# One tuned kernel, two parallel layers: loading the first 256 row pairs of A's input by plain copies with TensorE transposes, issuing the Q and K weight loads from SyncE, cutting the last odd rows in two column pieces, and new ranks

## The chip, the cores and the metric

The kernel runs on one core of one Trainium2 chip. The metric is the device time of one execution in microseconds (us). A kernel is run several times; the text quotes medians. Each execution also has a state. It is called slow when its granted TensorE clock is visibly below that of the other runs, or when it takes over 1.5% longer than the fastest run of the same kernel. Comparisons use fast runs only, and a difference under 2% counts as "same".

Engines in the profile: PE is TensorE's matmuls, PEld its weight loads, DVE is VectorE, ACT ScalarE, POOL GpSimd, SP SyncE (which here issues most of the DMAs). PSUM is the memory that TensorE writes; "evacuating" a PSUM tile means that VectorE or ScalarE copies it out, after which the buffer is free again.

## The reference

Two independent layers over 2048 rows of 448 columns, side by side in the output.

```python
def A(x, wqkv, wo):                 # x [1, 2048, 448], 16 heads of 28
    q, k, v = split(x @ wqkv)
    idx = pos[:, None] - 2 * arange(8)[None, :]        # 8 keys, every second row back
    logits = einsum("bhsd,bhswd->bhsw", q, k[idx]) * 28 ** -0.5      # masked where idx < 0
    return einsum("bhsw,bhswd->bhsd", softmax(logits), v[idx]) @ wo

def B(x, Lambda, B, C, log_dt, Dskip):                 # a linear recurrence, 448 states
    Lam_bar = exp(exp(log_dt) * Lambda)
    h[t] = Lam_bar * h[t - 1] + ((Lam_bar - 1) / Lambda * B) @ x[t]
    return 2 * real(C @ h) + x * Dskip

out = concatenate([A(...), B(...)], axis=-1)           # bfloat16
```

## The kernel before

Rows are handled as 1024 pairs: one row of the working layout holds an even and an odd row of x, 896 values. Matmuls need x with its columns on the partitions, so `xA` holds x transposed, seven slabs of 128. All of it came by DMA transposes, 128 row pairs at a time ("a tile" below), issued by SyncE. V and Q/K are products of two row-tiled matmuls that run side by side: "a pair".

```python
    def xbar_x(dst, src, lo, hi):
        SP.dma_start_transpose(dst[:, :, lo:hi], src[lo:hi, :])
    # ...
    xbar_x(xA, xA2, 0, 128)                                # x tile 0, transposed by the DMA
    ACT.dma_start(Wv[:, 0:3, :], wmain(2))                 # V's weights
    ACT.dma_start(Wv[0:64, 3, :], A_wqkv[384:448, 2 * D:3 * D])
    ACT.dma_start(Wraw[0:64, 3, :], A_wqkv[384:448, 0:2 * D])
    # ... small parameters
    for i in range(1, 4):
        xbar_x(xA, xA2, 128 * i, 128 * i + 128)
    ACT.dma_start(Wraw[:, 0:3, D:2 * D], wmain(1))         # K's weights, from ScalarE
    # ...
    ACT.dma_start(Wraw[:, 0:3, 0:D], wmain(0))             # Q's weights
    # ...
    def n_vw(e):                                           # copies of Wv for the second row tile
        V.tensor_copy(Wv[64:128, 3, :], Wv[0:64, 0, :])
        V.tensor_copy(Wv[0:64, 4:7, :], Wv[64:128, 0:3, :])
        V.tensor_copy(Wv[64:128, 4:7, :], Wv[0:64, 1:4, :])
    # ...
    def evac(e, o, i):                                     # from PSUM, on either engine
        if e == "A":
            ACT.copy(o, i)
        else:
            V.tensor_copy(o, i)
    # ... the last odd rows of B (t == 7): one PSUM unit, two halves of columns
        def half(e, lo, hi, h=h):
            evac(e, h["o"][:, 1, lo:hi], h[1][:, 1, lo:hi])
        # ...
        n3 = [node(f"ye{t}{1 + i}", {"AV"[i]: 0.3}, lambda e, i=i, half=half: half(e, 224 * i, 224 * i + 224), [n1, n2], r, frees=[(n1, 0)])
              for i in range(2)]
    # ... and before everything, a warm-up of TensorE with throw-away matmuls
    for i in range(11):
        PE.matmul(ps[:, 0, :], zz[:, 0:128], zz[:, 128:640], start=True, stop=True)
```

The order of the instructions is not written by hand. Every piece of work is a node with a cost on each engine that can do it; a small list scheduler runs through the nodes at build time, always taking the ready node with the lowest rank, and thereby fixes each engine's order and which engine evacuates what. The 22 pairs of numbers in `RANK` tune it.

## Time and profile before

| | before |
|---|---|
| median of the first three runs | 135.64 us (135.48 to 136.37) |
| span of the profiled execution | 136.1 us |
| time of that same execution | 138.0 us, state slow, mean granted clock 0.983 |
| TensorE busy in it | 127.0 us (93%) |

How to read it: TensorE is the busiest engine, so whatever leaves it idle, or makes it run at a lower clock, is what a change can gain. The prediction below shows the slices and stretches.

```profile
span 136.1 us, 3771 instructions
```

The span covers less than the timed duration (a later fast run: 133.9 against 135.86, about 2 less). A span of 136.1 is therefore an execution of about 138, and no run of the three quoted took that long.

### The profile page before, as it was taken

Reading aid. Unit: us, or ns where it says so; the run is one execution under the profiler, and the core shown is the slowest. Engines: PE = TensorE matmul, PEld = TensorE weight load, DVE = VectorE, ACT = ScalarE, POOL = GpSimd, SP = SyncE. Lnnn points to the kernel's source line nnn. Section 1 sums busy time; section 2 is a strip of 40 time slices with the busy share of each in tenths; the row PEclk is TensorE's granted clock in tenths of the full one; section 3 lists DMA queues with packets and bytes.
Section 4 is the critical chain, followed back from the end, with each engine's and each line's share of the span. In section 5 each row is a group of like instructions: output and inputs, shape, how many; then the busy total and the mean of one; then the engine's idle time right before and its main releaser. Section 6 shows DMA issues by size and latency. Waiting matters only on the chain.

```text
span 136.1 us, 3771 instructions
## 1 busy us (share of the span) xinstructions
PE 127.0 (93%) x1516; PEld 70.3 (52%) x1516; DVE 107.5 (79%) x191; ACT 88.2 (65%) x118; POOL 28.6 (21%) x109
## 2 busy tenths in 40 slices
PE   6849999999997999999999999999999999999980
PEld 2214567987434545445454545655666545455540
DVE  0505999999899799999999999999999999811110
ACT  0024999997999687699997889836766257511120
POOL 6965316401589900000000000000000010000000
PEclk9977999999999999999999999999999999999998
DMA  3999999791648939333313340089254765432121
GB/s 92 249 183 310 262 113 201 156 127 35 135 90 145 241 69 193 66 88 62 92 37 89 75 99 5 0 232 167 101 141 105 159 187 196 153 135 72 67 101 43
DMA packets 43938, 17.26 MB, mean 127 GB/s; under 512 B 35214, under 2 KB 43918, under 8 KB 43918
## 3 DMA queue, kind: packets, MB, share of 16 engines
q1 hardware_dynamic: 42448, 15.78, 53.7%
q10 hardware_dynamic: 1374, 1.21, 3.6%
q8 instruction: 13, 0.21, 0.7%
q14 instruction: 7, 0.06, 0.1%
q0 software_dynamic: 96, 0.00, 0.1%
HBM read 3.62 MB, written 3.67 MB: 54 GB/s over the span
## 4 chain that ended last, share of the span: by engine, by line
PE 72%; ACT 10%; DVE 7%; DMA 5%; issue 3%; SPq 1%; ACTq 0%
PE mm L528 21%; PE mm L778 14%; PE mm L970 8%; PE mm L979 8%; PE mm L737 5%; DMA xA<-in_A_x_dram 5%; PE mm L972 4%; PE mm L869 4%; PE mm L714 3%; PE mm L718 2%; ACT P L724 2%; DVE Va L507 2%; ACT wtmp L511 2%; ACT Kt L505 1%; ACT tab L454 1%
## 5 line engine op out<-in xcount | busy, mean ns | idle before, releaser
L724 ACT ACTIVATE P<-mm 128x896 bf16<-128x896 f32 (+1 forms) x36 | 31.4, 930 | 2.0 <-PE mm L718 1.9
L505 ACT CAST ys<-mm 128x896 bf16<-128x896 f32 (+2 forms) x16 | 12.2, 779 | 22.3 <-PE mm L979 8.9
L528 PE MATMUL mm<-xA,Wpad 64*128 64x256 bf16 (+1 forms) x168 | 26.4, 305 | 0.2 <-ACT Va L505 0.2
L529 PE MATMUL mm<-xA,Wpad 64*128 64x256 bf16 (+1 forms) x168 | 26.5, 305 | 0.0
L536 POOL MEMSET tick<- 1x1 f32 x40 | 5.0, 124 | 85.8 <-PE mm L529 85.6
L778 PE MATMUL mm<-xB,WT 128*128 128x512 bf16 x98 | 22.5, 379 | 0.5 <-ACT P L724 0.3
L528 PEld LDWEIGHTS <-Wpad 64*128 64x128 bf16 x168 | 15.3, 94 | 7.0 <-POOL tick L536 0.2
L528 PE MATMUL mm<-Wv,xA 64*128 64x448 bf16 x56 | 13.4, 378 | 2.5 <-DMA xA<-in_A_x_dram 2.2
L529 PEld LDWEIGHTS <-Wpad 64*128 64x128 bf16 x168 | 15.0, 94 | 0.8 <-issue 0.6
L778 PEld LDWEIGHTS <-WT 128*128 128x128 bf16 x98 | 9.1, 97 | 11.1 <-issue 0.9
L529 PE MATMUL mm<-Wv,xA 64*128 64x448 bf16 x56 | 13.4, 379 | 0.0
L970 PE MATMUL mm<-C,h 128*128 128x448 bf16 x56 | 11.9, 353 | 0.0
L979 PE MATMUL mm<-C,h 128*128 128x448 bf16 x56 | 11.9, 353 | 0.0
L528 PE MATMUL mm<-wo,OT 64*128 64x448 bf16 x56 | 10.8, 349 | 0.0
L529 PE MATMUL mm<-wo,OT 64*128 64x448 bf16 x56 | 10.8, 349 | 0.0
L744 DVE TENSOR_TENSOR O<-mm,rcs 112x896 bf16<-112x896 f32 (+1 forms) x9 | 9.8, 1092 | 0.3
L528 PEld LDWEIGHTS <-xA 64*128 64x128 bf16 x56 | 5.3, 100 | 7.3 <-DMA xA<-in_A_x_dram 3.2
L807 DVE TENSOR_TENSOR_SCAN rs<-p_r,ini,rv 128x512 bf16<-128x512 f32 x7 | 8.7, 1272 | 0.0
L737 PEld LDWEIGHTS <-P 128*128 128x128 bf16 x288 | 8.1, 96 | 1.3 <-issue 0.4
L1004 DVE TENSOR_TENSOR ys<-mm,xd 128x448 bf16<-128x448 f32 x3 | 1.9, 625 | 8.5 <-ACT ys L505 8.5
L807 DVE TENSOR_TENSOR_SCAN rs<-p_r,rv 128x512 bf16<-128x512 f32 x7 | 8.3, 1215 | 0.0
L505 ACT CAST u<-mm 128x1024 bf16<-128x1024 f32 (+1 forms) x6 | 5.2, 870 | 4.7 <-PE mm L778 4.5
(172 smaller groups left out, 243.0 us busy)
## 6 DMA issues: line engine op xcount, KB each, us to landing
out_dram<-ys SPq DMA_DIRECT2D x15, 224.0 KB, 2.4
Wraw<-in_A_wqkv_dram ACTq DMA_DIRECT2D x2, 336.0 KB, 5.2
wo<-in_A_wo_dram SPq DMA_DIRECT2D x2, 336.0 KB, 3.4
vw<-Va SPq DMA_DIRECT2D x2, 203.0 KB, 3.0
vw<-Va SPq DMA_DIRECT2D x2, 174.0 KB, 4.9
Wv<-in_A_wqkv_dram ACTq DMA_DIRECT2D x1, 336.0 KB, 3.4
natW<-in_B_B_re_dram SPq DMA_DIRECT2D x1, 336.0 KB
natW<-in_B_B_im_dram SPq DMA_DIRECT2D x1, 336.0 KB, 5.2
```

The lines of the kernel that those rows point to most:

```text
L505: ACT.copy(o, i)
L528: x = PE.matmul(ps[:, a, 0:n], lhs(0, lo[i]), rhs(0, lo[i]), start=(i == 0), stop=(i == 6), skip_group_check=True)
L529: y = PE.matmul(ps[:, b, 0:n], lhs(64, hi[i]), rhs(64, hi[i]), start=(i == 0), stop=(i == 6), skip_group_check=True)
L724: ACT.activation(P[:].rearrange("p s g q -> p g s q")[:, 2 * z:2 * z + 2, :, 0:n], h["s"][z][:, :, 0:4 * n].rearrange("p g (s q) -> p g s ...
L737: PE.matmul(av[:, par, 29 * hd:29 * hd + 29], hb_[par]["P"][:, hd // 4, hd % 4, :], v[:, par, hd, :], start=True, stop=True)
L744: V.tensor_tensor(O[0:n, :].rearrange("p (a h d) -> p a h d", a=2, h=H), avv[0:n, :, :, 0:DH], rc.unsqueeze(3).to_broadcast((n, 2, H, DH)) ...
L778: PE.matmul(ps[:, i, :], WT[:, j, 128 * m:128 * m + 128], xB[:, j, HALF * hf:HALF * hf + HALF], start=(j == 0), stop=(j == 6))
L807: V.tensor_tensor_scan(h["s"][:, i], p["r2"][:, k:k + 1].to_broadcast((128, HALF)), h["v"][:, i], 0.0 if hf == 0 else ini[:, m:m + 1], ALU ...
L869: PE.matmul(ps[0:n, i, 0:D], natW[:, m, D + 128 * k:D + 128 * k + n], lazy["C1"][:, m, :], start=(m == 0), stop=False, skip_group_check=True)
L970: PE.matmul(ps[:, 0, 0:D], hb[:, m, lo:lo + 128], lazy["C2"][:, m, :], start=(m == 0), stop=False, skip_group_check=True)
L972: PE.matmul(ps[:, 0, 0:D], xB[:, k, tk], Gm[:, k, :], start=False, stop=(k == 3), skip_group_check=True)
L979: PE.matmul(ps[:, 1, 0:D], hb[:, m, lo + 1:lo + 129], lazy["C1"][:, m, :], start=(m == 0), stop=(t in YD and m == 6), skip_group_check=True)
```

## The change

Its intent: the first stage of TensorE's work starts sooner and has no hole, because the first two tiles of x come by plain loads and TensorE, idle then anyway, transposes them; the K and Q weights leave ScalarE's queue, so that it has nothing to issue when evacuations start; and at the end less work follows the last matmul. All 22 ranks were retuned with it, and the warm-up falls from eleven matmuls to seven.

```diff
-    xbar_x(xA, xA2, 0, 128)
+    xn_ = [Pb[i][:].rearrange("p a b c -> p (a b c)")[:, 0:2 * D] for i in range(2)]
+    SP.dma_start(xn_[0], xA2[0:128, :])
     ACT.dma_start(Wv[:, 0:3, :], wmain(2))
     ACT.dma_start(Wv[0:64, 3, :], A_wqkv[384:448, 2 * D:3 * D])
-    ACT.dma_start(Wraw[0:64, 3, :], A_wqkv[384:448, 0:2 * D])
+    SP.dma_start(xn_[1], xA2[128:256, :])
 # ... (small parameters)
-    for i in range(1, 4):
+    for i in range(2, 4):
         xbar_x(xA, xA2, 128 * i, 128 * i + 128)
-    ACT.dma_start(rows[7:14, :], B_Lambda_re.rearrange("(c p) -> c p", p=64))
-    ACT.dma_start(Wraw[:, 0:3, D:2 * D], wmain(1))
-    for i in range(4, 6):
-        xbar_x(xA, xA2, 128 * i, 128 * i + 128)
-    ACT.dma_start(Wraw[:, 0:3, 0:D], wmain(0))
-    for i in range(6, 8):
+    SP.dma_start(Wraw[0:64, 3, :], A_wqkv[384:448, 0:2 * D])
+    SP.dma_start(Wraw[:, 0:3, D:2 * D], wmain(1))
+    xbar_x(xA, xA2, 512, 640)
+    SP.dma_start(Wraw[:, 0:3, 0:D], wmain(0))
+    for i in range(5, 8):
         xbar_x(xA, xA2, 128 * i, 128 * i + 128)
 # ... (B's x in two transposes instead of four; Wv's copies split into three nodes)
+    def n_xt(e, i, h):
+        h["ps"] = unit()
+        tp = h["tp"] = h["ps"][:].rearrange("p a b -> p (a b)").bitcast(BF16)
+        for k in range(7):
+            PE.transpose(tp[:, 1024 * (k // 4) + 128 * (k % 4):1024 * (k // 4) + 128 * (k % 4) + 128], xn_[i][:, 128 * k:128 * k + 128], eye[:])
+
+    def n_xe(e, i, z, h):
+        n = (4, 3)[z]
+        evac(e, xA[:, 4 * z:4 * z + n, 128 * i:128 * i + 128],
+             h["tp"][:, 1024 * z:1024 * z + 128 * n].rearrange("p (k n) -> p k n", k=n))
 # ... (nodes and dependencies for these; all 22 ranks)
+        def piece(e, lo, n, ds, tk=tk, h=h):
+            ps, hb = unit(), hbuf(1)
+            h["z", lo] = ps
+            for m in range(7):
+                PE.matmul(ps[:, 1, 0:n], hb[:, m, 385:513], lazy["C1"][:, m, lo:lo + n], start=(m == 0), stop=False, skip_group_check=True)
+ # ... (the skip term)
-            def half(e, lo, hi, h=h):
-                evac(e, h["o"][:, 1, lo:hi], h[1][:, 1, lo:hi])
+            for i, (lo, n, ds) in enumerate(((0, 320, (0, 1, 2)), (320, 128, (3,)))):
 # ... (piece, evacuation on VectorE or ScalarE, store, for each)
-    for i in range(11):
+    for i in range(7):
         PE.matmul(ps[:, 0, :], zz[:, 0:128], zz[:, 128:640], start=True, stop=True)
```

## The prediction

> **What bounds the kernel now.** I read the page first: engine totals and the 40 slices.
>
> ```profile
> PE 127.0 (93%) x1516; PEld 70.3 (52%) x1516; DVE 107.5 (79%) x191; ACT 88.2 (65%) x118; POOL 28.6 (21%) x109
> ...
> PE   6849999999997999999999999999999999999980
> DVE  0505999999899799999999999999999999811110
> ACT  0024999997999687699997889836766257511120
> PEclk9977999999999999999999999999999999999998
> ```
>
> TensorE is nearly full from slice 4 (13.6 us) to the end. VectorE and ScalarE are full only from slices 4 and 5 on, and PEclk has its one dip in slices 2 and 3. So the time is TensorE's work plus what is lost in the first 12 us and after its last matmul. Next, stretches of the start (TensorE busy, clock, DMA share, GB/s) and of all later time.
>
> ```profile
> 1.32:5.20 3.88, 3.88 (x10) 1.00 0.90 199
> 5.20:6.16 0.96, 0.52 (x4) 1.00 1.34 231
> 6.16:7.10 0.94, 0.93 (x8) 1.00 1.24 205
> 7.10:8.89 1.79, 0.00 (x0) 0.89 1.17 143
> 8.89:11.50 2.61, 2.61 (x14) 0.50 1.26 271
> ```
> ```profile
> 12.00:18.00 6.00, 6.00 (x72) 3.44 (x70) 5.62 (x27) 5.31 (x10) 1.86 (x9) 1.00 1.03 268
> 18.00:24.00 6.00, 5.60 (x88) 4.44 (x85) 5.85 (x18) 5.67 (x12) 2.75 (x12) 1.00 1.09 151
> 24.00:40.00 16.00, 16.00 (x223) 10.97 (x219) 15.32 (x26) 15.10 (x20) 6.16 (x28) 1.00 0.61 108
> 40.00:45.00 5.00, 4.16 (x36) 1.90 (x34) 4.64 (x7) 4.01 (x5) 4.92 (x15) 1.00 0.80 143
> 45.00:118.00 73.00, 72.75 (x997) 39.40 (x996) 70.35 (x109) 53.87 (x68) 4.20 (x22) 1.00 0.49 115
> ```
>
> The first 11 matmuls (1.32 to 5.7) are a dummy warm-up. The first V half-tile, four row-tiled pairs, runs at 6.16; then TensorE waits until 8.89 for the second x tile; then seven pairs run at clock 0.50, spaced 0.37 us and not 0.19. After 11.78 everything is at full clock. By then only 11 pairs are done, worth 11 x 0.19 = 2.1 us. Later idle is 0.40 + 0.84 + 0.25 = 1.5 us. From 12 to 40 us VectorE (0.95 to 0.97) and ScalarE (0.89 to 0.95) are nearly as full as TensorE: the start must move for all three. The end is the chain of waits, in order of time:
>
> ```profile
> 130.42 1.33 PE mm L979 x7
> 131.75 0.03 PE mm L982
> 131.78 0.18 PE mm L984 x3
> 131.96 0.02 issue
> 131.98 0.35 ACT ys L505
> 132.34 0.02 issue
> 132.36 0.39 DVE ys L507
> ```
>
> Two halves of one result, evacuated one after the other, 0.79 us after the last matmul; then the store and the end, to 136.1.
>
> **What the Trainium skill says.** (1) "TensorE: Matmul & The Clock Gate", Part 1 (The HAM clock gate): the array starts at half clock, a free-running window of about 3.4 us decides, and the phase varies from run to run. The trace agrees: warm-up matmuls of 512 columns are 0.43 us apart, the clock is full from about 5.1, lost during the 1.8 us gap and back at 11.8, steps of about 3.4 us. (2) The same page, Part 4 (PE-mode transpose): the result lands in PSUM and must be copied, and transposes do not count as busy for the clock as matmuls do. Before has just two tiny transposes, so nothing tests that. (3) "DMA: Bandwidth & Descriptors", Issuing engines are not separate DMA queues: moving a load to another issuer saves only issue time. The DMA share of 1.17 to 1.34 above agrees that the load is in the engines. (4) "PSUM — Partial Sum Buffer", PSUM bank collisions: two engines may not use one bank at once, so it has to be guarded by bank. The VectorE half starting 0.03 us after ScalarE's ends (132.33, 132.36) agrees.
>
> **Part 1: x tiles 0 and 1.** Removed: two DMA transposes of 1.3 us issue each and the wait to 8.89. Added: two plain loads (issue about 0.5 each, as the weight loads), 14 TensorE transposes, four evacuations. Seven dummies end at 1.32 + 7 x 0.43 = 4.3. Wv, issued at 0.81, landed at 4.24; x tile 0 should land about then too. Seven 128-column transposes at half clock cost 7 x 0.43/4 = 0.75: done at 5.1, tile 1 at 5.5 to 5.9. The instruction order says: ScalarE copies 512 columns (0.59 by its 512-column cast), then VectorE 384. Its casts of 224 and 896 columns (0.39, 1.09) give 1.04 ns a column, so 0.56. That gives 5.2 + 0.59 + 0.56 = 6.4 for tile 0. The first V half runs from 6.4 to 7.2, no earlier than before. VectorE then still has two Wv copies (about 0.2 + 0.8) and tile 1's 384 columns (0.56) ahead of the second half: 6.4 + 1.6 = 8.0. From there ten pairs x 0.19 finish tiles 0 and 1 at about 10.0. Before, those 14 pairs ended at 11.78 + 3 x 0.19 = 12.35. **Gain about 2.4 us on TensorE**, if the clock stays full. The first evacuation moves from 12.62 to about 9.5 on ScalarE (3.1) and from 11.73 to about 10.0 on VectorE (1.7), mean 2.4 also. The four added copies (about 1.1 us on each) lie ahead of that, in idle time. The added transposes replace four dummies (4 x 0.43 = 1.7).
>
> **Part 2: weights and x order on SyncE.** K's weights move from 4.24 on ScalarE's queue to about 5.2 on SyncE's (0.8, two plain loads, two transposes, one small load), Q's from 8.87 to about 7.5. Landing took 4.3 to 6.0 us, so K lands at 9.5 to 11.2. V of tiles 0 to 3 (28 pairs) ends at about 12.65; K's padding costs VectorE 1.6 and ScalarE 3.0 before K's first matmuls, so they come at about 12.5 to 13: it may cost TensorE 0 to 0.5. The later x transposes leave about 0.3 earlier, so x is not the limit. B's x in two pieces of 256 saves about 1 us of issue, wanted only near 37: hidden.
>
> **Part 3: last odd rows.** Columns are the same, only more matmuls: 7 x (320 + 128) columns, as 1.33 us before, plus four skips of 0.21, with a second set of seven weight loads hidden beside: 1.55 to 1.6 against 1.54. After the last matmul one ScalarE cast of 128 columns follows: 0.35 - 96 x 0.83 ns = 0.27, in place of 0.79. But the first piece's store (ready at about 132.0, issue 0.53) holds SyncE until 132.5, so the last store leaves 0.25 to 0.3 sooner, and it is 32 KB, not 112. **Gain 0.3 to 0.5.**
>
> **Sum:** 2.4 - 0.25 + 0.4 = 2.55 at a full clock. The new ranks reorder the mid-part: the sequence on TensorE near 40 us is the same, but the third softmax pair's neighbours on ScalarE differ. Of the 1.5 us of later idle I allow 0.5 to go and 0.3 to come: +0.2.
>
> **Rivals.**
> (a) The clock falls or does not rise. Only 3.0 us of dummies run ahead of transposes, and the window after 5.1 has gaps (about 0.5 and 0.8 us). Before, a window of 3.4 us with 0.52 + 0.93 = 1.45 busy lost it. If the same comes, nine pairs or so run at 0.37 and 1 to 1.7 us are lost, partly behind the wait for K: time near 134.1. I give this three in ten.
> (b) VectorE and ScalarE, and PSUM buffers, become the bound from 12 to 40 us. Four buffers hold V tiles 2 and 3 and the parameter transpose until evacuated behind the padding; then only VectorE's 1.7 survives: 135.64 - 1.7 - 0.4 = 133.5. For it: 0.95 and more busy; against: ScalarE starts 3.1 sooner and shares the evacuations.
> (c) DMA: Wv and x tile 0 compete, tile 0 lands late, each us late is one lost. Against: 199 GB/s in that stretch, while 271 was reached with transposes later.
> (d) Better than worked: tile 1's copy is quicker, the mid idle vanishes: 132.
>
> **Range and chances.** The working case is 135.64 - 2.75 = 132.9; (a) and (b) pull it up, (d) down; weighted I take 133.0. A gain over 2% means under 132.93, almost my middle, so the chances are nearly even: 0.47 faster, 0.51 within, 0.02 slower (all three parts failing at once). Range 131.7 to 134.4.
>
> **What would show it.** Step 1: first V pair at 6.2 to 6.6, second half at about 8.0, first V evacuation at about 9.5, spacing 0.19 with clock 1.00 between 8 and 12 (0.37 and 0.5 would be rival a). Step 2: K's first matmuls at 12.5 to 13 with no DMA wait over 0.5. Step 3: under 0.35 us from last matmul to last evacuation. Mid-part: the stretch from V tile 3 to the last matmul within 0.5 us of before. A gain in the start that is not there at 45 us would be rival b; a late first transpose, rival c.

## The result

| | before | after |
|---|---|---|
| median, same chip | 135.94 us (135.48 to 136.37) | 134.26 us (134.15 to 134.41) |
| ratio | | 0.988 (95%: 0.984 to 0.992), "same" |
| span of a fast execution | 133.9 us | 132.4 us |

A ratio is the mean time of the kernel's fast runs over the mean of the fast runs of before in the same rounds, so it is not quite the quotient of the medians. Repeated, the kernel after came to 134.26 us and 0.990 (0.987 to 0.993).

The gain is real, about 1.4 to 1.7 us, and smaller than the 2.75 that the prediction worked out (2.6 after it weighed the rivals). The time lies inside its range of 131.7 to 134.4 and in its likelier class. The page of the kernel after (engine totals, then slices of 3.3 us):

```profile
PE 126.1 (95%) x1533; PEld 71.1 (54%) x1533; DVE 107.4 (81%) x193; ACT 90.2 (68%) x121; POOL 27.7 (21%) x108
...
PE   5899999999999999999999999999999999999980
...
DVE  0439999899879999999999999999999899921130
ACT  0639899989998956999999899834775266211120
...
PEclk9999999999999999999999999999999999999999
```

TensorE, ScalarE and VectorE are full one or two slices sooner, and the dip in PEclk is gone. But a dip is no property of the kernel before either. Stretches of TensorE in a **fast** execution of the unchanged kernel before (columns: stretch, its length, PE busy with number of matmuls, granted clock, DMA share, GB/s):

```profile
1.32:7.52 6.20, 4.77 (x19) 1.00 1.05 223
7.52:12.00 4.48, 4.17 (x44) 1.00 1.21 303
12.00:24.00 12.00, 11.60 (x172) 1.00 1.03 192
...
38.00:43.00 5.00, 4.16 (x39) 1.00 0.88 159
```

The same stretches of the kernel after:

```profile
1.32:7.52 6.20, 5.67 (x32) 1.00 0.95 236
7.52:12.00 4.48, 4.48 (x47) 1.00 1.13 231
12.00:24.00 12.00, 11.48 (x170) 1.00 0.98 215
...
38.00:43.00 5.00, 5.00 (x81) 1.00 0.87 153
```

The hole at 7 to 9 us and the half clock behind it, on which the prediction built its largest term, are not there in the fast run of before. From 7.52 us on, the change takes out 0.31 us of idle time in the second stretch and 0.84 us at 38 to 43 us; the prediction had seen an idle time of that size there, but allowed only 0.2 net for all of the middle. In the third stretch it even adds a little. The same as a table of moments (us from the start of the span):

| | before, the slow run that the prediction read | before, fast | after |
|---|---|---|---|
| first pair of V | 6.16 | 6.32 | 6.21 |
| first full pair on x tile 1 | 8.89 | 7.52 | 7.44 |
| 15th pair of V | 12.41 | 10.04 | 9.21 |
| first scores | 35.92 | 33.55 | 33.70 |
| third group of scores | 45.36 | 42.98 | 41.88 |
| last matmul ends | 132.04 | 129.85 | 128.72 |
| span | 136.1 | 133.9 | 132.4 |

Between the fast runs the account of 1.5 us is: 0.83 gained by the 15th V pair, 0.98 lost until the first scores, 1.25 gained at 38 to 43, nearly nothing after that until the last matmul (1.13 in all), and the rest, 0.3 to 0.4, in the tail (spans are printed to 0.1 us).

The 0.83 is not all owed to the earlier x. In this fast run of before, TensorE loses 0.60 us between two V pairs (8.67 to 9.46) to two small transposes of parameters and to a wait for a small GpSimd instruction ("tick"):

```profile
9.46 0.36 PE L528 MATMUL mm<-Wv,xA 64*128 64x448 bf16 x1 [0.31 <-POOL tick L536]
```

The kernel after runs the same two transposes later, at 11.51, and loses 0.23 to them. So by the 28th V pair (12.50 and 12.03) only 0.47 of the 0.83 is left. Where tile 1 lands late the front is worth more: in the fast profile of experiment 2 the 15th pair came at 10.85.

The tail of the chain of waits of the kernel after, in order of time:

```profile
128.19 0.39 PE mm L1014 x7
128.58 0.07 PE mm L1017
128.65 0.02 issue
128.67 0.27 ACT ys L523
```

One small copy, 0.27 us, is all that follows the last matmul.

### The profile page after: what moved, and what is told of

Read it like the earlier page. It is cut to its first block, busy times and chain, and to the rows that moved or that the text cites.

```text
span 132.4 us, 3803 instructions
## 1 busy us (share of the span) xinstructions
PE 126.1 (95%) x1533; PEld 71.1 (54%) x1533; DVE 107.4 (81%) x193; ACT 90.2 (68%) x121; POOL 27.7 (21%) x108
## 4 chain that ended last, share of the span: by engine, by line
PE 88%; ACT 4%; DVE 4%; issue 2%; POOL 0%; POOLq 0%; ACTq 0%
PE mm L546 27%; PE mm L804 17%; PE mm L996 8%; PE mm L1003 7%; PE mm L763 5%; PE mm L998 5%; PE mm L895 4%; PE mm L740 4%; PE mm L547 3%; PE mm L744 3%; PE mm L1055 2%; PE mm L1014 1%; ACT wtmp L529 1%; DVE Va L525 1%; ACT P L750 1%
## 5 line engine op out<-in xcount | busy, mean ns | idle before, releaser
L546 PE MATMUL mm<-xA,Wpad 64*128 64x256 bf16 (+1 forms) x168 | 27.2, 305 | 0.4 <-POOL tick L554 0.4
L547 PE MATMUL mm<-xA,Wpad 64*128 64x256 bf16 (+1 forms) x168 | 27.2, 306 | 0.1
L523 ACT CAST ys<-mm 128x896 bf16<-128x896 f32 (+2 forms) x15 | 11.3, 764 | 23.1 <-PE mm L1003 8.9
L546 PEld LDWEIGHTS <-Wpad 64*128 64x128 bf16 x168 | 14.9, 94 | 8.9 <-POOL tick L554 1.4
L547 PEld LDWEIGHTS <-Wpad 64*128 64x128 bf16 x168 | 14.7, 94 | 1.2 <-issue 0.5
L547 PE MATMUL mm<-Wv,xA 64*128 64x448 bf16 x56 | 12.4, 350 | 0.1
L546 PE MATMUL mm<-Wv,xA 64*128 64x448 bf16 x56 | 12.5, 350 | 0.0
L996 PE MATMUL mm<-C,h 128*128 128x448 bf16 x56 | 11.9, 353 | 0.0
L1003 PE MATMUL mm<-C,h 128*128 128x448 bf16 x49 | 10.4, 353 | 0.0
L523 ACT CAST u<-mm 128x1024 bf16<-128x1024 f32 (+1 forms) x8 | 7.2, 903 | 3.2 <-PE mm L804 3.2
L815 DVE TENSOR_TENSOR ra<-u,tab 128x2048 bf16<-128x2048 bf16 x6 | 7.3, 1221 | 0.7 <-DVE h L841 0.5
```

Of the source, the lines that this page charges most:

```text
L546: x = PE.matmul(ps[:, a, 0:n], lhs(0, lo[i]), rhs(0, lo[i]), start=(i == 0), stop=(i == 6), skip_group_check=True)
L547: y = PE.matmul(ps[:, b, 0:n], lhs(64, hi[i]), rhs(64, hi[i]), start=(i == 0), stop=(i == 6), skip_group_check=True)
L815: V.tensor_tensor(a[:], x[:].unsqueeze(1).to_broadcast((128, 2, 2, HALF)), tab[:, :, k, :].unsqueeze(2).to_broadcast((128, 2, 2, HALF)), A ...
L996: PE.matmul(ps[:, 0, 0:D], hb[:, m, lo:lo + 128], lazy["C2"][:, m, :], start=(m == 0), stop=False, skip_group_check=True)
L1003: PE.matmul(ps[:, 1, 0:D], hb[:, m, lo + 1:lo + 129], lazy["C1"][:, m, :], start=(m == 0), stop=(t in YD and m == 6), skip_group_check=True)
```

## The experiments

All outputs are right. Theory at the start: the front gain is small because the profile of before was a slow run. Rival: the gain was there but VectorE and ScalarE swallowed it before the scores.

### 1. The kernel before again (before_again)

No edit: a second execution with a profile.

> The kernel before, unchanged, for a profile in the fast state. The profile that the prediction was read from is of a run of 138.0 us, 2.1 over the median, and is marked slow. Theory A (the lost clock from 8.9 to 11.8 us belongs to that slow run alone): a fast profile has a span of about 134.0 us, no stretch at clock 0.5 in the first 12 us, pairs spaced 0.19 us there, and from 12 us on the same distances as in the slow one. Rival B (the clock is lost in every run and the slow run lost its 2 us elsewhere): the fast profile shows clock near 0.5 between 8.9 and 11.5 us again, and is 2 us shorter somewhere after 12 us. The ratio to before is 1.00 either way.

Measured: 135.83 us, ratio 1.002 (0.998 to 1.005), profile of a fast run, span 133.9 with clock 0.999. The line of the timeline with the first matmul on x tile 1 (start, duration, idle time before it and what ended it):

```profile
7.52 0.36 PE L528 MATMUL mm<-Wv,xA 64*128 64x448 bf16 x1 [0.27 <-DMA xA<-in_A_x_dram]
```

The same place in the slow run of before:

```profile
8.89 0.55 PE L528 MATMUL mm<-Wv,xA 64*128 64x448 bf16 x1 [1.81 <-DMA xA<-in_A_x_dram]
```

The DMA transpose of tile 1 landed 1.4 us later in the slow run, and the matmuls behind it took 0.55 to 0.58 and not 0.36 us. So the loss that the prediction wanted to remove occurs in some executions only.

### 2 and 3. The tail alone (tail_only), and everything but the tail (no_tail)

```diff
  # tail_only: before, with
+        def piece(e, lo, n, ds, ...): ...        # and its nodes; no other hunk
  # no_tail: after, with
-        def piece(e, lo, n, ds, ...): ...        # back to two halves of one unit
```

> The kernel before with only the last odd rows in two column pieces. The prediction gave this part 0.3 to 0.5 us. The two traces (last matmul to end of span: about 4.1 us before, 3.8 us after) agree with that: time 0.3 to 0.5 us under before, ratio 0.9965 to 0.998. Rival: the second piece's seven extra weight loads and the second store take it back: ratio 1.00.

> The changed kernel with only the two column pieces undone: the start and the queues alone. If the parts add up, time is 1.2 to 1.4 us under before (ratio 0.990 to 0.991), the changed kernel being 1.66 under. If the start gives nothing by itself and the tail carries the gain, ratio 0.998 to 1.00.

Measured: tail_only 135.57 us, ratio 0.999 (0.996 to 1.001); no_tail 134.87 us, 0.993 (0.990 to 0.995), beside 135.68 for before. The spread of before hides 0.2 us, but the traces agree with each other: from the last matmul to the end of the span it is about 4.0 us in before and in no_tail, 3.7 in after. In tail_only it is 4.1 all the same: its last copy ends 0.21 us after the last matmul, as in after, but from there to the end it took 0.4 longer. By the ratios the tail is worth 0 to 0.5 us and the rest 0.6 to 1.4.

The profiled execution of tail_only took 136.3 us, near the upper end of before's fast runs, and shows why these differ:

```profile
8.71 0.36 PE L528 MATMUL mm<-Wv,xA 64*128 64x448 bf16 x1 [1.54 <-DMA xA<-in_A_x_dram]
```

Tile 1 was again late, nearly as late as in the slow run, but here the clock stayed full: the matmul takes 0.36 us. The 0.65 us that its last matmul is later than in experiment 1 come from this. So before has executions with tile 1 early, with tile 1 late, and with tile 1 late and the clock lost, at spans of 133.9, 134.6 and 136.1. That all the spread of its fast runs (135.3 to 136.4) comes from there is likely, but three profiles don't show it. In the six profiles with after's front, TensorE waited 0 to 0.9 us for the plain load of tile 1, against 0.27, 1.54 and 1.81 for the DMA transpose in these three.

### 4. Filling the hole with throw-away matmuls (before_filled)

```diff
-    for i in range(11):
+    for i in range(13):
 # and, ahead of the V matmuls on x tile 1 (b == 1):
+                for i in range(8 if b == 1 else 0):
+                    PE.matmul(h["ps"][:, 0, :], zz[:, 0:128], zz[:, 128:640], start=True, stop=True)
```

> The kernel before with two more dummy matmuls in the warm-up (13) and eight dummies (8 x 0.21 us = 1.7 us) between the first and the second V half, so that TensorE does not stand still while it waits for x tile 1; nothing useful added. If the clock is lost in that gap in most runs of before, worth 7 pairs x 0.18 us = 1.3 us, time falls by about 1.3 us. Theory A (lost in the slow runs only): the median is equal to before within 0.3 us, and no run is as slow as 138.0. Were the dummies longer than the wait, it would be slower by up to 0.4 us.

Measured: 137.17 us, ratio 1.011 (1.008 to 1.013), a miss. The clock was never lost and the six runs lie within 0.47 us of each other, but tile 1's V began at 9.30 instead of 7.52, and the last matmul ended 1.34 later. Eight fillers cost 1.7 us each time; the hole they fill was 0.27 us in before_again and 1.54 in tail_only. It is also the first sign that a delay of TensorE at 8 us largely reaches the end (1.34 of 1.78).

### 5. The kernel after again (after_again)

No edit.

> The changed kernel, unchanged, on the chip of this batch, so that the variants below have a partner with more runs: ratio to before 0.9878 measured, 0.984 to 0.992; the difference of the two fast profiles (133.9 and 132.4 us) is 1.5 us, ratio 0.989.

Measured: 134.26 us, 0.990 (0.987 to 0.993). The milestones repeat those of the first profile within 0.17 us. Runs of after lie between 134.1 and 134.7, those of before beside them between 135.3 and 136.3.

### 6 and 7. The ranks of one kernel in the other (old_ranks, new_ranks)

```diff
 # old_ranks: after, with before's
+RANK = {"vi": (-263.4, 62.011), "v": (-254.81, 47.21), ...
 # new_ranks: before, with after's
+RANK = {"vi": (-544.75, 131.055), "v": (-110.39, 34.569), ...
```

> The changed kernel with the 22 ranks of before. Theory A: of the 1.13 us that the fast profiles differ at the last matmul, the start gives 0.83 at V tile 3 but none is left at the first score group (33.55 before, 33.70 after); what is left comes from the 1.2 us of waits on ScalarE's exp near 39 us, which the new order takes away. With old ranks those waits return and the time is that of before, ratio 0.997 to 1.003. Rival B: the start pays by itself, the ranks are noise: ratio about 0.988 to 0.990 as with the new ranks.

> The kernel before with only the ranks of after. Theory A in its strong form (ranks alone make the gain): 0.990 to 0.993. Theory A in its weak form (ranks were fitted to the new start and need it): 1.00 or slower, because the old start orders V and Q differently under them. Rival B: 1.00 with the waits near 39 us unchanged.

Measured: 149.23 us, 1.099, and 151.28 us, 1.114: both far outside what was expected. In both, part of the loss is the clock: its mean was 0.954 and 0.959 in the profiles. The biggest waits of TensorE in old_ranks, beyond the start (what waits, for what, total, times, longest):

```profile
PE mm L740 <- ACT u L523: 2.3, 1, 2.3
PE mm L740 <- ACT P L750: 2.0, 1, 2.0
PE mm L740 <- DVE O L770: 1.8, 1, 1.8
```

And in new_ranks:

```profile
PE mm L970 <- DVE h L814: 7.3, 1, 7.3
```

The first scores came at 31.16 us in old_ranks, 2.5 sooner than in after, and the time was still 15 us longer. A rank set is tuned to one set of nodes, and the experiment can't separate "the ranks' share" of the gain. It says that the change and its ranks are one thing.

### 8. The weight loads issued from ScalarE (weights_act)

```diff
-    SP.dma_start(Wraw[0:64, 3, :], A_wqkv[384:448, 0:2 * D])
-    SP.dma_start(Wraw[:, 0:3, D:2 * D], wmain(1))
+    ACT.dma_start(Wraw[0:64, 3, :], A_wqkv[384:448, 0:2 * D])
+    ACT.dma_start(Wraw[:, 0:3, D:2 * D], wmain(1))
     xbar_x(xA, xA2, 512, 640)
-    SP.dma_start(Wraw[:, 0:3, 0:D], wmain(0))
+    ACT.dma_start(Wraw[:, 0:3, 0:D], wmain(0))
```

> The changed kernel with the three Q and K weight loads issued by ScalarE, in the same program order, everything else the same (the order on TensorE, VectorE is identical). The loads of K then no longer stand behind the x transposes on SyncE (K issued at 5.65 us there). If K's landing holds the padding (it starts at 9.77 on ScalarE, 10.66 on VectorE, TensorE loses 0.8 us at 12.2 to 13.5), earlier weights bring the first K matmul (12.22) forward by up to 0.8 us and the time down by 0 to 0.5. If VectorE's V evacuation (9.54 to 10.63), not the landing, holds it: no change within 0.2 us, or slower if the wait for the load queue delays ScalarE's own evacuations or the x tiles.

Measured: 140.2 us, ratio 1.032 (1.028 to 1.037), a miss by a wide margin. ScalarE's timeline in the first 10 us (issues are those of its queue, ACTq):

```profile
4.82 0.48 ACTq L298 DMA_DIRECT2D Wraw<-in_A_wqkv_dram  x1
5.81 0.40 ACTq L299 DMA_DIRECT2D Wraw<-in_A_wqkv_dram  x1
7.12 0.40 ACTq L301 DMA_DIRECT2D Wraw<-in_A_wqkv_dram  x1
7.55 1.28 ACT L523 ACT_TABLE_LOAD   x1 [7.55 <-DMA xA<-in_A_x_dram]
8.84 1.07 ACT L523 COPY xA<-mm 128x512 bf16<-128x512 bf16 x2
```

ScalarE now copies the transposed x out of PSUM (at 5.28 in after), but its queue holds the three loads ahead of that, and these wait, with gaps, to be issued. Behind them the table load (1.28 us), which in after ran at 3.19 while ScalarE was idle, is in the way too. The copy comes at 8.84, and the first V pair at 9.48 instead of 6.21:

```profile
9.48 0.55 PE L546 MATMUL mm<-Wv,xA 64*128 64x448 bf16 x1 [2.71 <-ACT xA L523]
```

The clock has not risen by then (0.55 us a matmul; the transposes before the wait took 0.95 and 0.93, as at half clock), and V's pairs stay 0.37 us apart until 13.58. The last matmul ends at 133.77, 5.05 later than in after: 3.27 by the late start, nearly all the rest by the clock. So moving the weights to SyncE was no detail of the change: with x coming through ScalarE's hands the two parts need each other.

### 9. Giving the front's gain back (start_back)

```diff
+                for i in range(4 if b == 1 else 0):
+                    PE.matmul(h["ps"][:, 0, :], zz[:, 0:128], zz[:, 128:640], start=True, stop=True)
```

This is put ahead of the V matmuls on x tile 1 in the kernel after, 4 x 0.21 = 0.84 us.

> The kernel after with four throw-away matmuls (4 x 0.21 = 0.84 us at full clock) just ahead of the second half of V, so that TensorE gives back the 0.83 us by which the 21st V pair is earlier in the profile of the kernel after than in a fast profile of the kernel before. Theory A (the start of TensorE bounds all that follows, so the front's gain reaches the end one for one): the last matmul ends 0.6 to 0.9 us later than in the kernel after, time about 134.9 to 135.1 against 134.26. Theory B (the start's gain is swallowed at the first group of scores, which starts at 33.55 before and 33.70 after, because VectorE and ScalarE set it; the 1.5 us come from waits on ScalarE that went away near 39 us): first group of scores unmoved, time 134.2 to 134.5. Part of the 0.84 can hide in the 0.27 us that TensorE waits for tile 1 anyway, so 0.5 us is the least that A allows.

Measured: 135.38 us (134.99 to 135.54) beside 136.22 for before, whose runs were slower and more spread (three of twelve slow); ratio 0.994 (0.991 to 0.997). First scores in after, then in this kernel:

```profile
33.70 0.39 PE L740 MATMUL mm<-msk 32*128 32x512 bf16 x4
```
```profile
34.67 0.40 PE L742 MATMUL mm<-msk 32*128 32x512 bf16 x4
```

The first scores move by 0.97, the last matmul by 1.26, the time by 1.1 against after's 134.26 (by the ratios, 0.6 to 0.8). **Theory B is refuted, A holds**: a delay at the start of TensorE reaches the end about one for one. TensorE's work has the same order in the two kernels, so it can be matched one by one: it is 0.96 us late from the full pairs on x tile 1 to 60 us, and 1.25 from 62 on; the last 0.3 is not explained. (The 15th V pair came at 10.29, so this run gave back 0.25 more than the front's gain: in this execution the first V pair was already 0.35 late.) ScalarE and VectorE are nearly as full as TensorE from 12 to 40 us, but what they do is evacuate what TensorE makes, so they move with it: ScalarE's first exponentials start at 36.16 in after and at 37.13 here.

### 10. The same delay behind V (pe_late)

```diff
-        tp = hold["tp"] = unit()[:].rearrange("p a b -> p (a b)").bitcast(BF16)
+        u = unit()
+        for i in range(4):
+            PE.matmul(u[:, 0, :], zz[:, 0:128], zz[:, 128:640], start=True, stop=True)
+        tp = hold["tp"] = u[:].rearrange("p a b -> p (a b)").bitcast(BF16)
```

> The kernel after with the same four throw-away matmuls (0.84 us), now behind the V pairs, just ahead of the transposes of the small parameters at about 11.3 us. If TensorE's own queue is what holds the first Q and K matmul at 12.2 us, everything behind is 0.84 us later and the time is about 135.0. If what holds it is VectorE's and ScalarE's padding of the weights (they run until 12.5 and 12.7 us, and TensorE waits 0.25 and 0.54 us in that stage), most of the 0.84 is absorbed: last matmul at most 0.3 us later, time 134.3 to 134.5. That would show that the front's gain beyond some 0.5 us could not have been worth anything, whatever the size the prediction gave it.

Measured: six runs at 135.14, 135.16, 135.19, 135.98, 136.81 and 137.32, ratio of the fast ones 0.997 (0.992 to 1.002). The three quick ones are 0.9 above after: in sum the delay is not absorbed here either. The execution with the profile was the slowest. It tells what happened (stretches as above, from the first V pair):

```profile
6.69:10.40 3.71, 3.71 (x22) 1.00 1.04 257
10.40:12.00 1.60, 1.60 (x20) 1.00 1.25 151
```

The pairs are 0.37 us apart until 10.40 and soon 0.19 (ten pairs in 3.71 us; from 10.67 on eight in 1.5 us), though the column of the granted clock says 1.00 all along: the trace of this execution holds no clock record before 10.56, and the view takes that as full speed. Up to here this kernel gives TensorE the same work as after. **The prediction's rival (a) exists**: with seven warm-up matmuls the clock is not always up when V starts.

The same profile shows that the padding does hold the first K matmul in after: there the first full K pair starts at 12.58, 0.55 us after V's last pair, here at once (14.90 to 15.09, the usual 0.19). So 0.36 of the 0.84 is absorbed at this place; in this execution much of it is lost again later (0.31 at 23.68 to 23.99).

### 11. One GpSimd wait taken out (pool_early)

In after, TensorE waits 0.41 us at 22.6 for a small GpSimd instruction that is queued behind constant fills. GpSimd's fills are moved forward among GpSimd's own instructions; the order on the other four engines is unchanged.

```diff
+        for x, y in (("one0", "q121k"), ("one1", "q111k"), ("zer0", "v4k"), ("zer3", "q131k"), ("zer2", "q131k"), ("zer1", "q131k"), ("rcs", "q001k")):
+            m = next(n for n in order if n["name"] == x)
+            order.remove(m)
+            order.insert(next(i for i, n in enumerate(order) if n["name"] == y) + 1, m)
```

> The kernel after with GpSimd's constant fills moved ahead among GpSimd's own instructions, so that the tick that TensorE waits 0.41 us for at 22.6 to 23.2 us isn't queued behind them; the order on the four other engines is the same. If TensorE bounds the stretch up to the scores, the last matmul ends 0.3 to 0.4 us earlier and the time is 133.85 to 134.0 (ratio to the kernel before 0.987); if VectorE and ScalarE set the scores' start, the wait only moves and the time is 134.2 to 134.3.

Measured: 134.65 us, ratio 0.991 (0.986 to 0.997), six runs in two clusters, 134.15 to 134.30 and 135.0 to 135.96. The trace: here V started 0.32 later than in after's profile (again a clock that rose late, at 7.16), K 0.23 later; the wait at 22.6 is gone, another at 20.6 is 0.1 to 0.2 longer, and the last matmul ends at 128.73 against 128.72. So the edit won back about 0.25 us in this one execution, but the quick cluster is no quicker than after's runs. Inconclusive, and no better version.

### 12. One warm-up matmul instead of seven (few_dummies)

```diff
-    for i in range(7):
+    for i in range(1):
```

> The kernel after with one warm-up matmul instead of seven. The prediction's first rival was the clock: that the transposes put where warm-up matmuls had been leave TensorE at half clock. If warm-up matmuls are what raises the clock, V pairs run 0.37 us apart instead of 0.19 for the first 3 to 4 us, second half of V starts 1 to 2 us later and the time is 135.3 to 136.5. If the transposes themselves raise it as well as matmuls do (they start at about 4.3 us, the first V pair at 6.2), the V pairs are 0.37 apart for only the first 1 to 2 us, time 134.6 to 135.2. If the warm-up is worth nothing, 134.2 to 134.4.

Measured: 135.79 us, ratio 0.998 (0.994 to 1.003). From the first V pair on:

```profile
6.80:10.08 3.28, 3.28 (x20) 1.00 1.05 263
10.08:12.00 1.92, 1.92 (x24) 1.00 1.19 211
```

Nine pairs in 3.28 us (0.37 apart) and then ten in 1.9 (0.19). The fourteen transposes from 3.76 to 6.88 us, with 1.25 us idle between them, did not raise the clock; it rose after some 3.3 us of real matmuls. The first scores are 1.70 later than in after and the last matmul 1.70 later: one for one again. The warm-up that the change kept is worth about 1.5 us (1.2 to 1.4 by the ratios), as much as the whole change.

## Why the prediction was right or wrong

**The time and the class came out right; the working that led there did not.**

*The baseline* is the step that failed. "Before, those 14 pairs ended at 11.78 + 3 x 0.19 = 12.35 [...] Gain about 2.4 us on TensorE" was read from an execution of 138.0 us, and the gain was then taken from 135.64, the median of runs that had no such loss. In a fast run of before the 15th pair starts at 10.04, and the gain at this place is 0.83 (experiment 1). The 2.2 us of span between the slow and the fast profile are about what the sum took off a median that never held them. The hint was on the page: a span longer than the median time.

*The end of the 14 pairs in the kernel after* was mis-sized in the other direction, which hid part of that. The prediction has "from there ten pairs x 0.19 finish tiles 0 and 1 at about 10.0"; the runs have 9.2. First cause: VectorE's copy of 384 columns was priced with its casts from float32, 0.56 us; it took 0.36 and 0.33. The source is bfloat16 here. The Trainium skill ("VectorE: DVE Perf Modes", Why PSUM operands drop a tier) says that a PSUM operand allows up to twice the base rate, and float32 only the base rate. The trace agrees: after a fixed part of about 0.16, 0.36 us for 384 columns is 0.52 ns a column, half the 1.04 of the float32 casts. Second cause: VectorE's last two copies of Wv took 0.8 us and not 1.0, and V on tile 1 did not wait for the whole of it: its first matmul ran at 6.98, and full pairs from 7.44 and not 8.0.

*The K stage* was to cost 0 to 0.5 us. Its matmuls began at 12.22, slightly before the predicted 12.5 to 13, with no wait for a DMA, as predicted. But TensorE lost 0.25 us at 12.22 to 12.58 (VectorE's padding) and 0.54 at 12.81 to 13.46, of which the trace names 0.27 to GpSimd:

```profile
12.92 0.27 PE L547 MATMUL mm<-xA,Wpad 64*128 64x256 bf16 x1
13.46 0.28 PE L546 MATMUL mm<-xA,Wpad 64*128 64x256 bf16 x1 [0.27 <-POOL tick L554]
```

That is 0.79, and 0.41 follow at 22.6 (experiment 11). Before has gaps of its own between the 15th V pair and the first scores, so these are not simply the 0.98: summed from start to start, less the usual spacing, it loses 0.9 us there (two waits of 0.36 and 0.38 at 17.3 and 19.6, and smaller ones), and after 1.8, of which 0.23 for the two small transposes that before had already run. The difference of 0.9 is most of the 0.98 by which the kernel after falls behind. In experiments 9 and 12 after's gaps were of the same length although TensorE came 1 and 1.7 us later, so they depend on TensorE's own progress and not on a fixed time of a weight load. For VectorE's padding experiment 10 agrees: delayed behind V, TensorE no longer waited for it. For the wait at 13.46 this was argued from the equal lengths, not tested by taking the wait away.

*The middle* got "+0.2" for all of what the new ranks do. It held the largest single gain, 1.25 us. In the fast run of before TensorE waits twice for ScalarE's exponentials near 39 us:

```profile
PE mm L714 <- ACT P L724: 0.5, 1, 0.5
PE mm L778 <- ACT P L724: 0.3, 1, 0.3
```

After has neither. ScalarE's queue before (the table of sines, a table load, the exponentials):

```profile
30.67 1.91 ACT L448 ACTIVATE tab<-tmpB 128x2048 bf16<-128x2048 f32 x1
...
36.59 1.28 ACT L724 ACT_TABLE_LOAD   x1
37.88 3.77 ACT L724 ACTIVATE P<-mm 128x1024 bf16<-128x1024 f32 x4
```

And after:

```profile
28.48 1.91 ACT L451 ACTIVATE tab<-tmpB 128x2048 bf16<-128x2048 f32 x1
...
34.87 1.28 ACT L750 ACT_TABLE_LOAD   x1
36.16 1.94 ACT L750 ACTIVATE P<-mm 128x1024 bf16<-128x1024 f32 x2
```

The exponentials come 1.72 sooner after scores that are 0.15 later; the sines no longer stand behind three evacuations that wait for TensorE, which is read from the traces and not tested alone. In start_back, with the front's gain given back and the order kept, the waits stay away. With the front more than cancelled (0.25 too much at the 15th V pair), the order and the tail leave 0.2 us in the spans of fast profiles (133.9 and 133.7), so some 0.45 without that excess, and 0.8 (0.4 to 1.3) in the ratio; the front carries the rest. What of the order is due to the ranks and what to ScalarE's earlier start couldn't be separated (experiments 6 and 7).

*The tail* was right: "0.27, in place of 0.79" is what the trace has, and the 0.3 to 0.4 us in the spans lie in the predicted 0.3 to 0.5; in times, tail_only shows 0.2 (-0.1 to 0.5), which leaves room for nothing at all.

*The rivals.* (a), the clock, did not occur in the two profiles of after, but of the six profiles with after's first 6 us of TensorE work unchanged (after, after_again, no_tail, start_back, pool_early, pe_late) one had it in full (pe_late) and one in part (pool_early). Of the 34 runs of these kernels, 7 lie 0.8 us or more above the fastest of their kernel; without a profile the cause of most of them stays open. The Trainium skill says in Part 1 of "TensorE: Matmul & The Clock Gate" that the deciding window is free-running, so that its phase differs from run to run; the clock records of these six traces start at 4.6, 5.8, 6.3, 6.4, 7.1 and 10.6 us, which fits. (b) is refuted by experiments 9 and 12, and by the times of 10. (c) did not occur: the second tile's transposes waited 0.42 us, and the first V pair came at 6.21 where 6.4 was predicted. (d) happened in part: the copies were quicker and the idle time near 39 us vanished.

So 133.0 erred by 1.3 us. Against the account of the fast profiles the sum had 1.6 too much gain at the front (2.4 against 0.83), 0.7 too little loss up to the scores (0.25 against 0.98) and 1.05 too little gain in the middle (0.2 against 1.25), which nets to 1.25. That three errors of 0.7 to 1.6 us partly cancelled, and that the range was wide enough for the remainder, was luck.

## What to carry to other kernels

Before a loss in a profile is sized, ask whether the profiled run is typical: compare its span with the median time, and its clock and landing times with a second profile. Where TensorE is the bound, a delay at its start is paid in full at the end, even if other engines look equally full; so transposes put in place of warm-up matmuls, and loads queued on an engine that also evacuates, are priced first. And when a change comes with a new instruction order, expect a large part of the gain or loss where the order changed rather than where the diff is.

## What the Trainium skill lacked or had wrong

- "TensorE: Matmul & The Clock Gate" gives an idle window of about 3.4 us as what puts the clock down; elsewhere it says only that frequent short idle times in one kernel made the clock oscillate, without their length. Here an idle gap of 1.81 us ahead of tile 1 (and one of 0.44 us shortly before) was followed by half speed in one execution (0.55 us a matmul), and one of 1.54 us was not in another (0.36). Gaps well under a window can cost the clock.
- The same page, Part 4, says that transposes don't count as busy in the same way; few_dummies fits that: fourteen transposes, then still half speed for 3.28 us. It is no proof, as they filled only 1.9 of 3.1 us. What the page lacks: transposes themselves run faster once the clock is up. Seven in a row took 0.93 to 0.95 us at half clock and 0.56 in after_again.
- "DMA: Bandwidth & Descriptors", Issuing engines are not separate DMA queues, counts only the issue time for the choice of issuer. In weights_act three issues of 0.40 to 0.48 us, with gaps between them and a table load of 1.28 us behind, held back ScalarE's first copy from 5.28 to 8.84 us, and the time was 3.2% over that of before: an issuer's other work belongs in that section.
- On no page: the time before the first recorded clock change stands as 1.00 in these profiles, whatever the clock was. In few_dummies and pe_late pairs 0.37 us apart stand under a clock of 1.00; the spacing of equal matmuls is the safer reading.
